# A planner that lays out two attentions on one core: its model of transfers changed, four output products ready at the end, and the V product of the first unit at other places

## The chip, the cores and the metric

The kernel runs on one core of one Trainium2 chip. The metric is the device time of a whole execution, in microseconds; the median of several executions is given with its lowest and highest. One execution was also recorded by the hardware profiler. Its span, from the first to the last recorded instruction, is a little shorter than the time of that execution.

## The reference

Two independent attentions over their own inputs, each with S = 2048 tokens, D = 1024 and 32 heads of 32 dimensions. A looks at eight keys at distances 0, 2, ..., 14 behind each query; B at the 256 keys up to and including the query. The outputs stand side by side.

```python
# A: W, dil = 8, 2
idx = pos[:, None] - (jnp.arange(W) * dil)[None, :]
kg, vg = k[:, :, idx_c, :], v[:, :, idx_c, :]
logits = jnp.where(idx >= 0, einsum("bhsd,bhswd->bhsw", q, kg) * Dh ** -0.5, -1e9)
a = einsum("bhsw,bhswd->bhsd", softmax(logits), vg) @ wo
# B: W = 256
mask = (i - j >= 0) & (i - j < W)
scores = jnp.where(mask, einsum("bhqd,bhkd->bhqk", q, k) * Dh ** -0.5, -1e9)
b = einsum("bhqk,bhkd->bhqd", softmax(scores), v) @ wo
return jnp.concatenate([a, b], axis=-1)
```

In both, q, k and v are thirds of x @ wqkv, and everything is float32.

## The kernel before, in words

**Units and slots.** The work is cut into eight units of 512 tokens. Units 0 to 3 are the chunks of B ("dense"; units 1 to 3 also need the last 256 keys of the unit before, called the halo). Units 4 to 7 are A: its tokens are sorted into even and odd, so that a step of two becomes a step of one and the window is 8 neighbouring keys; two chunks for each parity, the second of each with a halo. Each unit has eight slots of four heads (a slot's running number is hg = 8u + s).

**Arithmetic.** Float32 products are made on TensorE from two parts of each operand (a value cast to fp32r, and what the cast left), in three products (TERMS): high by high, high by low, low by high. So a weight is loaded raw (L103), cast on DVE (L129) and its rest is made by a subtraction on DVE (L137) or POOL (L134). This is the class Stream. It has three raw buffers (NRAW) and walks a fixed list of items; split_to(n) splits up to item n, and the next load is issued when a split is planned to end. An item "x" is split into two halves in xpool, an item "w" as one tile in wpool, which has three buffers. The first eight loads are issued by ACT, the others by POOL.

**A slot** runs through these steps:
1. the products for q and k (L363, 24 matmuls each), their copies out of PSUM (ACT L314 and DVE L318 into one of two buffers nat), and SP's copies of them into the stacked operands qst and kst (L328: three for q, three for k; halo copies L308 and L333). There are two of each stack; so the copies of slot hg are issued only after the last product of slot hg − 2 (dictionary `waiting`);
2. the first pass over the scores (L614, 16 matmuls), the row maximum on DVE (L619) and the sum of exponentials on ACT (L624);
3. the logarithm (L637), three small steps on DVE (up to L645), the rows' constants turned round on TensorE (L653), copied on DVE (L657) and put by SP (L660) into two more rows of qst;
4. the second pass (L696 dense, L509 window), which now gives scores less the constant, the exponentials on ACT (L701 or L514), the masks on POOL and DVE (L682, L685, L520, L524);
5. the product with V (L741 or L548), and the copy of its result into ot (ACT L577, DVE L581).

Beside them run the V product of the unit in four parts (L415, copied out through copy_out at L379 or L382) and the output product of the unit before in eight products (L455, n = 0 to 7), each copied into the one output buffer `ost` (pool stp, NST = 1) and stored by ACT (L470). V_SLOTS says after which slot's q and k products a part of V stands; O_SLOTS the same for output products. The last V part of a unit also holds the splits of the next unit's x. The last unit's output products come at the end, each over k = 0 to 7, where k needs ot of slot k; k = 7 has to wait for the last slot.

**PSUM.** Ring rg has three banks (L363, L415, L455), ring rs four (L614, L653, L696, L509), ring ro one (L741, L548).

**Order.** Everything is issued in an order that Python works out beforehand. The class Clock keeps a time at which each engine is free, and the durations given to its methods (0.95 for a stack copy, 1.9 for a raw load and so on) are estimates. The loop at L801 to L829 has four sequences: the row steps (aux), second passes with the product with V (twos), first passes (ones), and the large products (gemm). At each step it asks each sequence when its next item could start and takes the first; what follows an item (copies, masks, DMAs) is put off by `defer` to its planned time and issued in that order. So a duration in the Clock has no time on the chip, but shifts where instructions stand in the queues of the engines. Transfers have two planned queues, "copies" (from SP) and "loads" (from ACT and POOL); one that runs while the other queue is busy is made longer by half the overlap.

The tail is ordered by hand after that: the first TAIL = 2 of the last eight output products run up to k = 6, then their last steps, then the others.

Of the kernel before, what the change touches and what calls it, by code (L numbers as in the profile page):

```python
# [14 lines left out]
P = 128  # L15
NG = 8
NK = 8
# [6 lines left out]
VPARTS = ((0,2),(2,2),(4,2),(6,2))  # L24
V_SLOTS = {0: 0, 1: 1, 5: 2, 7: 3}
O_SLOTS = {2: (0, 1), 3: (2, 3), 4: (4, 5), 5: (6, 7)}
NX, NST = 10, 1
TAIL, LAND, XAT = 2, 0.45, 1
C1, C3, CG, CV = 0.114, 0.2, 0.231, 0.243
TERMS = ((0, 0), (0, 1), (1, 0))  # L30

# [1 line left out]
class Clock:  # L33
# [3 lines left out]
    SEM = 0.17  # L37

    def __init__(self):
        self.free = dict(pe=0.0, act=0.0, dve=0.0, pool=0.0, sp=0.0, copies=0.0, loads=0.0)  # L40
        self.later, self.lands = [], []
        self.n = 0

    @property
# [3 lines left out]
    def use(self, eng, dur, *ready):  # L48
        start = max((self.free[eng],) + ready)
        self.free[eng] = start + dur  # L50
        return start + dur + self.SEM

    def copy(self, dur, *ready):

        return self.move("copies", "loads", self.use("sp", 0.63, *ready, self.lane()) + 0.4, dur)

    def load(self, dur, *ready):

        return self.move("loads", "copies", self.use("act", 0.35, *ready, self.lane()) + 0.45, dur)

    def fetch(self, dur, *ready):

        t = max(self.use("pool", 1.0, *ready) + 0.6, self.free["loads"])
        self.free["loads"] = t + dur + 0.5 * max(0.0, min(2 * dur, self.free["copies"] - t))
        return self.free["loads"] + LAND

    def lane(self):

        return self.lands[-8] if len(self.lands) >= 8 else 0.0

    def move(self, q, other, t, dur):

        t = max(t, self.free[q])
        self.free[q] = t + dur + 0.5 * max(0.0, min(2 * dur, self.free[other] - t))
        self.lands.append(self.free[q] + LAND)
        return self.lands[-1]

    def defer(self, t, f):
        heapq.heappush(self.later, (t, self.n, f))
# [7 lines left out]
class Stream:  # L87
# [10 lines left out]
    def load_to(self, n):  # L98
        while self.loaded < min(n, len(self.items)):
            raw = self.raws.tile([P, 1024], F32, tag="raw", name="raw")  # L100
            ap = self.items[self.loaded][1]
            early = self.loaded < 8
            (self.nc.scalar if early else self.nc.gpsimd).dma_start(raw if len(ap.shape) == 2 else raw.rearrange("p (a b) -> p a b", a=2), ap)  # L103
            self.raw[self.loaded] = raw, (self.ck.load if early else self.ck.fetch)(1.9, self.ck.now)
            self.loaded += 1

    def split_to(self, n):
        while self.split < min(n, len(self.items)):
            i = self.split
            self.load_to(i + 1)  # L110
            raw, t0 = self.raw.pop(i)
            if self.items[i][0] == "x":
                self.tiles[i], self.ready[i] = [], []
                for h in range(2):
                    t = self.xpool.tile([P, 2, S], F32R, tag="x", name="x")
                    self.ready[i].append(self.parts(t, raw[:, h * S:(h + 1) * S], t0))
                    self.tiles[i].append(t)
            else:
                t = self.wpool.tile([P, 2, 1024], F32R, tag="w", name="w")
                self.ready[i] = self.parts(t, raw, t0)  # L120
                self.tiles[i] = t
            self.split += 1
            end = self.ready[i] if self.items[i][0] != "x" else max(self.ready[i])
            self.ck.defer(end, lambda n=i + NRAW + 1: self.load_to(n))

    def parts(self, t, raw, t0):
# [20 lines left out]
def kernel(ctx, tc, xs, wqk, wv, wo, outs, units):  # L147
# [23 lines left out]
    for u in range(U):  # L171
        for s in range(NG):
            if u and s in O_SLOTS:
                plan += [("o", u - 1, n) for n in O_SLOTS[s]]
            plan.append(("qk", u, s))
            if s in V_SLOTS:
                plan.append(("v", u, V_SLOTS[s]))
        if u + 1 < U:
            plan.append(("x", u + 1))
    plan += [("o", U - 1, n) for n in range(NG)]  # L180
# [14 lines left out]
    for p in plan:  # L195
        ly = units[p[1]][0]
        if p[0] == "o":
            item(p, "w", wo[ly, p[2]])
        elif p[0] == "v":
            s0, n = VPARTS[p[2]]  # L200
            for g in range(n):
                if n == 2:
                    item(p + (g,), "w", wv[ly, s0 + g])
                else:
                    w4 = wv[ly, s0 + g // 2:s0 + g // 2 + 3:2, :, g % 2 * 512:g % 2 * 512 + 512]
                    item(p + (g,), "w", w4.rearrange("t p c -> p t c"))
        elif p[0] == "qk":
            for t in range(2):
                if p + (t,) not in where:
                    item(p + (t,), "w", wqk[ly, 2 * p[2] + t])  # L210
        else:
            if NG - 1 in V_SLOTS:
                item(("qk", p[1], 0, 0), "w", wqk[units[p[1]][0], 0])
                unit_x(p[1])
            else:
                unit_x(p[1], 0)
                item(("qk", p[1], 0, 0), "w", wqk[units[p[1]][0], 0])
                unit_x(p[1], 1, 2, 3)
# [79 lines left out]
    def qk_items(u, s):  # L298
# [5 lines left out]
        def read_halo():  # L304
            w = 256 if dense else 128
            hb = halo[(u + 1) % 2][s]
            for r, a in enumerate((0, 1, 0)):
                nc.sync.dma_start(kst[buf][r:96:3, :, 256 - w:256].bitcast(F32), hb[:, a, 256 - w:])  # L308
                ck.copy(0.55 if dense else 0.35, ck.now)

        def evac(t, ps, bank):
            hl = natp.tile([P, 2, S], F32R, tag="nat", name="nat")
            sc = SCALE if t == 0 else 1.0
            nc.scalar.activation(hl[:, 0, :], ps, AF.Copy, scale=sc)  # L314
            r = ck.use("act", 0.48, ck.now + ck.SEM)

            def low():
                nc.vector.scalar_tensor_tensor(hl[:, 1, :], ps, sc, hl[:, 0, :].bitcast(F32), op0=ALU.mult,  # L318
                                               op1=ALU.subtract)
                e = ck.use("dve", 0.6, r)  # L320
                rg.give(bank, e)

                def stack():
                    if t == 1 and has_halo:
                        read_halo()
                    dst, c = (qst[buf], 0) if t == 0 else (kst[buf], 256)
                    for i, a in enumerate((0, 0, 1) if t == 0 else (0, 1, 0)):
                        nc.sync.dma_start(dst[i:96:3, :, c:c + S].bitcast(F32), hl[:, a, :].bitcast(F32))  # L328
                        e2 = ck.copy(0.95, e, ck.now)
                    if t == 1:  # L330
                        done["stack"][u, s] = e2
                    if t == 1 and u + 1 < U and units[u + 1][3]:
                        nc.sync.dma_start(halo[u % 2][s], hl[:, :, 256:].bitcast(F32))  # L333
                        e2 = ck.copy(0.95, e, ck.now)
                    done["nat"][hg, t] = e2

                if hg < 2 or hg - 2 in done["o"]:
                    stack()
                else:
                    waiting.setdefault(hg - 2, []).append(stack)  # L340

            ck.defer(r, low)
# [95 lines left out]
    def o_items(u, n):  # L438
        h = {}

        def ready(k):
            if (u * NG + k) not in done["ot"]:
                return None
            if k == 0:
                st.split_to(where["o", u, n] + 1)
                h["r"] = st.ready[where["o", u, n]]
                return latest(rg.when(), h["r"], done["ot"][u * NG])
            return done["ot"][u * NG + k]

        def run(k):  # L450
            if k == 0:
                h["ps"], h["b"] = rg.take()
                h["w"], _ = st.get(where["o", u, n])
            for i, (a, b) in enumerate(TERMS):
                nc.tensor.matmul(h["ps"], h["w"][:, a, k * P:(k + 1) * P], ot[u, k][:, b, :],  # L455
                                 start=(k == 0 and i == 0), stop=(k == NK - 1 and i == 2))
            if k == 3 and (u < U - 1 or n != TAIL - 1):
                st.split_to(where["o", u, n] + 2)

        def after(k):  # L460
            if k == NK - 1:
# [1 line left out]
                for f in list(stores.values()):  # L463
                    f()
                o = stp.tile([P, S], F32, tag="ost", name="ost")
                e = copy_out(o, h["ps"], h["b"], rg)

                def store():
                    if stores.pop((u, n), None):
                        nc.scalar.dma_start(outs[u, n], o)  # L470
                        ck.load(0.8, e)

                stores[u, n] = store
                ck.defer(e, store)
# [114 lines left out]
    def attention(u, s):  # L589
# [9 lines left out]
        def first(b, j):  # L599
# [18 lines left out]
            def top():  # L618
                nc.vector.tensor_tensor_reduce(ps[:, :n], ps[:, :n], mask[:, cut:full], scale=-1.0, scalar=BIG,  # L619
                                               op0=ALU.add, op1=ALU.min, accum_out=nm)  # L620
                e = ck.use("dve", (n + 80) / 960, ck.now)

                def total():
                    nc.scalar.activation(ps[:, :n], ps[:, :n], AF.Exp, bias=nm, scale=-1.0, accum_out=sm)  # L624
# [26 lines left out]
        def rows(hl):  # L651
# [4 lines left out]
            def copy():  # L656
# [1 line left out]
                e = ck.use("dve", 0.25, ck.now)  # L658
                rs.give(bank, e)
                nc.sync.dma_start(q[96:98, :, :].bitcast(F32), rt.bitcast(F32))  # L660
                h["rows"] = ck.copy(0.3, e)

            return copy

# [209 lines left out]
```

## Time and profile before

| | |
|---|---|
| median of 3 executions | 1975.59 us (1972.74 to 1976.52) |
| the profiled execution | 1973.82 us |
| its span | 1972.1 us |
| mean granted clock of TensorE | 0.987 of full speed |
| weight load / VectorE / ScalarE / GpSimd busy | 1619.8 / 1295.7 / 957.5 / 708.7 us |
| moved by DMA | 294.92 MB, mean 150 GB/s |

Busy shares by line: the costliest groups show how the work of TensorE is made up. Columns: line, engine, operation, tiles and count; then busy time and mean ns of one; then the idle time ahead of them and what ended most of it.

```profile
L363 PE MATMUL g<-x,w 128*128 128x512 f32 x3072 | 801.9, 401 | 8.6 <-DVE w L129 8.0
...
L415 PE MATMUL g<-w,x 128*128 128x256 f32 x3072 | 413.3, 285 | 0.0
...
L455 PE MATMUL g<-ot,w 128*128 128x512 f32 x1536 | 384.2, 397 | 3.6 <-DVE w L129 2.9
...
L614 PE MATMUL s<-kst,qst 96*128 96x384 f32 (+3 forms) x1024 | 238.7, 303 | 16.2 <-ACT s L624 7.1
```

Matmuls are pipelined, so the mean of one holds overlap: 24 matmuls of L363 in a row take 5.54 us, 0.231 each. The idle time stands in the last column. A time with a line behind it, as in "7.1 <-ACT s L624", says who ended most of that idle time: here TensorE waited for a bank of ring rs until ACT had summed the exponentials in it.

### The profile page before, as it was taken

The page shows a single profiled execution, that of the slowest core. Times are in us where ns is not written, and L with a number is a line of the kernel's source. Part 1 is how long each engine was busy: PE and PEld are TensorE (multiplying, and loading weights), DVE is VectorE, ACT ScalarE, POOL GpSimd, SP SyncE. Part 2 cuts the span into 40 slices and gives each one's busy share as a digit, 9 for nine tenths or more (in the row PEclk, how much of TensorE's full clock was granted, in tenths as well). Part 3 has the DMA queues.
Part 4 walks back from the last instruction along what each step waited for, and adds up shares of the span by engine and source line. Part 5 has one row for each costly group of instructions (what it writes and reads, how often), then busy time and mean ns, then how long its engine had stood idle before and what let it go on. Part 6 is the DMA issues. An engine that isn't in the chain of part 4 may idle for free.

```text
span 1972.1 us, 36479 instructions
## 1 busy us (share of the span) xinstructions
PE 1924.7 (98%) x12608; PEld 1619.8 (82%) x12608; DVE 1295.7 (66%) x3762; ACT 957.5 (49%) x3137; POOL 708.7 (36%) x923
## 2 busy tenths in 40 slices
PE   7999999999999999999999999999999999999998
PEld 6878887888877878788878888978888788888886
DVE  5687776678665786567865657655666557666653
ACT  3565554475654656555563344423534334434441
POOL 4334343444433434443443323233332333233221
PEclk9999999999999999999999999999989999999998
DMA  5555546455546465345645647455553565556442
GB/s 176 150 139 153 160 124 178 132 153 157 152 136 174 121 189 149 117 140 148 177 119 146 173 139 196 128 149 170 149 163 116 174 177 162 141 146 172 136 126 75
DMA packets 136502, 294.92 MB, mean 150 GB/s; under 512 B 14464, under 2 KB 42112, under 8 KB 136320
## 3 DMA queue, kind: packets, MB, share of 16 engines
q1 hardware_dynamic: 85632, 124.82, 26.1%
q0 software_dynamic: 40320, 146.82, 22.9%
q10 hardware_dynamic: 10368, 20.98, 2.9%
q8 instruction: 100, 1.64, 0.4%
q14 instruction: 82, 0.67, 0.1%
HBM read 163.58 MB, written 27.26 MB: 97 GB/s over the span
## 4 chain that ended last, share of the span: by engine, by line
PE 84%; DVE 7%; DMA 6%; ACT 2%; issue 1%; SPq 0%; POOL 0%; DVEq 0%; ACTq 0%; POOLq 0%
PE g L363 31%; PE g L455 16%; PE g L415 16%; PE s L614 7%; PE s L696 5%; PE o L741 4%; PE s L509 3%; DMA qst<-rt 3%; PE o L548 2%; DMA kst<-nat 1%; DMA raw<-xs 1%; DVE x L137 1%; DVE w L129 1%; ACT s L624 1%; DVE w L137 1%
## 5 line engine op out<-in xcount | busy, mean ns | idle before, releaser
L363 PE MATMUL g<-x,w 128*128 128x512 f32 x3072 | 801.9, 401 | 8.6 <-DVE w L129 8.0
L134 POOL TENSOR_TENSOR w<-raw,w 128x512 fp32r<-128x512 f32 x225 | 392.5, 1745 | 897.2 <-PE s L614 285.7
L363 PEld LDWEIGHTS g<-x,w 128*128 128x128 f32 x3072 | 562.0, 191 | 110.9 <-DVE w L129 8.4
L624 ACT ACTIVATE s<-s,nm 128x384 f32<-128x384 f32 (+3 forms) x1024 | 452.3, 443 | 231.0 <-DVE nm L619 227.1
L415 PE MATMUL g<-w,x 128*128 128x256 f32 x3072 | 413.3, 285 | 0.0
L415 PEld LDWEIGHTS g<-w,x 128*128 128x128 f32 x3072 | 392.7, 191 | 1.9 <-issue 0.6
L455 PE MATMUL g<-ot,w 128*128 128x512 f32 x1536 | 384.2, 397 | 3.6 <-DVE w L129 2.9
L455 PEld LDWEIGHTS g<-ot,w 128*128 128x128 f32 x1536 | 283.8, 190 | 58.1 <-DVE w L129 3.6
L619 DVE CUSTOM_DVE_ANT_0 s<-s,mask_d 128x384 f32<-128x384 f32 (+2 forms) x512 | 262.0, 556 | 72.9 <-PE s L614 71.5
L614 PE MATMUL s<-kst,qst 96*128 96x384 f32 (+3 forms) x1024 | 238.7, 303 | 16.2 <-ACT s L624 7.1
L701 ACT ACTIVATE pbuf<-s 128x384 f32<-128x384 f32 (+2 forms) x480 | 197.1, 507 | 85.5 <-PE s L696 81.8
L614 PEld LDWEIGHTS s<-kst,qst 96*128 96x128 f32 x1024 | 181.3, 192 | 60.5 <-ACT s L624 18.1
L624 ACT ACTIVATION_READ_ACCUMULATOR s<-s,nm 128x1 f32 x1024 | 210.2, 205 | 0.0
L619 DVE CUSTOM_DVE_ANT_0 s<-s,mask_w 128x136 f32<-128x136 f32 (+1 forms) x512 | 142.4, 322 | 98.4 <-PE s L614 96.8
L129 DVE CAST w<-raw 128x1024 fp32r<-128x1024 f32 x256 | 199.9, 781 | 9.4 <-PE g L455 9.4
L137 DVE TENSOR_TENSOR w<-raw,w 128x512 fp32r<-128x512 f32 x287 | 197.2, 696 | 8.8
L682 POOL TENSOR_SCALAR_AFFINE_SELECT pbuf<-pbuf 128x128 f32<-128x128 f32 (+1 forms) x383 | 147.9, 404 | 150.1 <-ACT pbuf L701 143.5
L314 ACT ACTIVATE nat<-g 128x512 fp32r<-128x512 f32 x128 | 76.6, 598 | 255.2 <-PE g L363 247.8
L318 DVE SCALAR_TENSOR_TENSOR nat<-g,nat 128x512 fp32r<-128x512 f32 x128 | 88.3, 690 | 145.5 <-ACT nat L314 134.9
L524 DVE TENSOR_TENSOR pbuf<-pbuf,keep_w 128x272 f32<-128x272 f32 (+1 forms) x224 | 116.9, 566 | 61.5 <-ACT pbuf L514 60.6
L619 DVE DVE_READ_ACCUMULATOR2_ANT nm<- 128x1 f32 x1024 | 144.3, 141 | 0.0
L696 PEld LDWEIGHTS s<-qst,kst 98*128 98x128 f32 x704 | 106.2, 189 | 37.8 <-PE o L741 10.0
(48 smaller groups left out, 1227.3 us busy)
## 6 DMA issues: line engine op xcount, KB each, us to landing
raw<-wqk POOLq DMA_DIRECT2D x126, 512.0 KB, 3.7
qst<-nat SPq DMA_DIRECT2D x192, 256.0 KB
kst<-nat SPq DMA_DIRECT2D x192, 256.0 KB
raw<-wo POOLq DMA_DIRECT2D x64, 512.0 KB, 3.7
raw<-wv POOLq DMA_DIRECT2D x62, 512.0 KB, 4.5
outs<-ost ACTq DMA_DIRECT2D x64, 256.0 KB
raw<-xs POOLq DMA_DIRECT2D x28, 512.0 KB, 4.8
halo<-nat SPq DMA_DIRECT2D x40, 256.0 KB
```

The lines of the kernel that those rows point to most:

```text
L129: nc.vector.tensor_copy(t[:, 0, :], raw)
L134: nc.gpsimd.tensor_tensor(o, a, b, op=ALU.subtract)
L137: nc.vector.tensor_tensor(o, a, b, op=ALU.subtract)
L363: nc.tensor.matmul(h["ps"], h["w"][:, a, k * P:(k + 1) * P], xt[u][k][:, b, :], start=(k == 0 and i == 0), stop=(k == NK - 1 and i == 2))
L415: nc.tensor.matmul(ps, xt[u][k][:, a, p0:p0 + P], h["w"][:, c, k % kw], start=(k == 0 and i == 0 and r == 0), stop=(k == NK - 1 and i == 2 ...
L455: nc.tensor.matmul(h["ps"], h["w"][:, a, k * P:(k + 1) * P], ot[u, k][:, b, :], start=(k == 0 and i == 0), stop=(k == NK - 1 and i == 2))
L614: nc.tensor.matmul(ps[:, :n], q[0:96, j, b * P:(b + 1) * P], kk[0:96, j, c0:c1], start=True, stop=True)
L619: nc.vector.tensor_tensor_reduce(ps[:, :n], ps[:, :n], mask[:, cut:full], scale=-1.0, scalar=BIG, op0=ALU.add, op1=ALU.min, accum_out=nm)
L624: nc.scalar.activation(ps[:, :n], ps[:, :n], AF.Exp, bias=nm, scale=-1.0, accum_out=sm)
L682: nc.gpsimd.affine_select(w, w, pattern=[[0, m], [step, n]], compare_op=ALU.is_ge, fill=0.0, base=base, channel_multiplier=chan)
L696: nc.tensor.matmul(ps[:, i * n:(i + 1) * n], kk[0:98, j, 256 + kb * P:256 + (kb + 1) * P], q[0:98, j, q0:q0 + n], start=True, stop=True)
L701: nc.scalar.activation(w, ps[:, :pack * n].rearrange("p (j n) -> p j n", j=pack), AF.Exp)
```

## The change

**1. The Clock's transfers.** The two planned queues are replaced by one list of busy stretches. A transfer asks for a start (the issue time plus a lead) and gets the first gap from there on that is long enough, except that it never goes ahead of one that asked for an earlier start; it runs alone, with no stretching. Every kind of transfer goes through it, the loads issued by POOL too. Their estimated durations change: a raw load 1.9 to 1.95, a stack copy 0.95 to 1.08, a halo copy of the window kind 0.35 to 0.45, the row copy 0.3 to 0.35, an output store 0.8 to 0.85. A load on POOL is planned to hold POOL for 0.6 instead of 1.0. The row maximum on DVE is planned as (n + 110) / 960 instead of (n + 80) / 960.

**2. Four output products ready at the end.** TAIL becomes 4. Product n = 3 of the last unit takes its bank from ring rs instead of rg. The weights of the last unit's products n = 3 to 7 become items "xw": they are split into two halves in xpool, with a planned time for each half. The places at which split_to is called in the last unit's products are set anew.

**3. V of the first unit.** Unit 0 has V parts after slots 0, 2, 4 and 7 (V0_SLOTS) instead of 0, 1, 5 and 7.

No product, copy or store is added or taken away, except that the five weights of "xw" are cast in two halves each.

```diff
+V0_SLOTS = {0:0,2:1,4:2,7:3}
 NX, NST = 10, 1
-TAIL, LAND, XAT = 2, 0.45, 1
+TAIL, LAND, XAT = 4, 0.45, 1
...
-        self.free = dict(pe=0.0, act=0.0, dve=0.0, pool=0.0, sp=0.0, copies=0.0, loads=0.0)
-        self.later, self.lands = [], []
+        self.free = dict(pe=0.0, act=0.0, dve=0.0, pool=0.0, sp=0.0)
+        self.later, self.lands, self.busy = [], [], []
...
+    def issue(self, eng, hold, lead, dur, *ready):
+        start = max((self.free[eng],) + ready)
+        self.free[eng] = start + hold
+        return self.move(start + lead, dur)
+
     def copy(self, dur, *ready):
-        return self.move("copies", "loads", self.use("sp", 0.63, *ready, self.lane()) + 0.4, dur)
+        self.lands.append(self.issue("sp", 0.63, 1.25, dur, *ready, self.lane()))
+        return self.lands[-1]
...
     def fetch(self, dur, *ready):
-        t = max(self.use("pool", 1.0, *ready) + 0.6, self.free["loads"])
-        self.free["loads"] = t + dur + 0.5 * max(0.0, min(2 * dur, self.free["copies"] - t))
-        return self.free["loads"] + LAND
+        return self.issue("pool", 0.6, 1.3, dur, *ready)
...
-    def move(self, q, other, t, dur):
-        t = max(t, self.free[q])
-        self.free[q] = t + dur + 0.5 * max(0.0, min(2 * dur, self.free[other] - t))
-        self.lands.append(self.free[q] + LAND)
-        return self.lands[-1]
+    def move(self, t, dur):
+        busy = self.busy = [x for x in self.busy if x[1] > self.now - 20.0]
+        i = 0
+        while i < len(busy):
+            if busy[i][1] <= t or busy[i][0] < t:
+                t = max(t, busy[i][1])
+            elif busy[i][0] - t >= dur:
+                break
+            else:
+                t = busy[i][1]
+            i += 1
+        busy.insert(i, (t, t + dur))
+        return t + dur + LAND
...
-            if self.items[i][0] == "x":
+            if self.items[i][0] != "w":
...
+            vs = V_SLOTS if u else V0_SLOTS
+            if s in vs:
+                plan.append(("v", u, vs[s]))
...
-            item(p, "w", wo[ly, p[2]])
+            item(p, "w" if p[1] < U - 1 or p[2] < 3 else "xw", wo[ly, p[2]])
...
-                        e2 = ck.copy(0.95, e, ck.now)
+                        e2 = ck.copy(1.08, e, ck.now)
...
+        last = u == U - 1
+        ring = rs if last and n == 3 else rg
...
+                h["r"] = r if isinstance(r, list) else [r, r]
+                return latest(ring.when(), h["r"][0], done["ot"][u * NG])
+            return max(done["ot"][u * NG + k], h["r"][k // 4])
...
-            if k == 3 and (u < U - 1 or n != TAIL - 1):
-                st.split_to(where["o", u, n] + 2)
+            if k == 3 and (not last or n == 0 or n > 2):
+                st.split_to(where["o", u, n] + (3 if last and n == 0 else 2))
+            if k == 5 and last and n in (1, 2):
+                st.split_to(where["o", u, n] + 3)
...
-                e = ck.use("dve", (n + 80) / 960, ck.now)
+                e = ck.use("dve", (n + 110) / 960, ck.now)
```

## The prediction

> **What bounds the kernel now.** I read the page's totals and its chain of waits first, then TensorE's waits, then windows around each wait, then the timeline.
>
> ```profile
> span 1972.1 us, 36479 instructions
> ...
> PE 1924.7 (98%) x12608; PEld 1619.8 (82%) x12608; DVE 1295.7 (66%) x3762; ACT 957.5 (49%) x3137; POOL 708.7 (36%) x923
> ...
> PE 84%; DVE 7%; DMA 6%; ACT 2%; issue 1%; SPq 0%; POOL 0%; DVEq 0%; ACTq 0%; POOLq 0%
> ```
>
> TensorE is busy 98%; 1972.1 − 1924.7 = 47.4 us are idle. The matmuls stay the same in kind and number, so only idle time, and what follows it, can change. TensorE's waits, with total, count and longest (us):
>
> ```profile
> engine line waited for: us in total, times, longest us
> PE g L363 <- DVE w L129: 8.0, 1, 8.0
> PE s L614 <- ACT s L624: 7.1, 8, 1.2
> PE s L509 <- DMA qst<-rt: 6.7, 10, 1.8
> PE s L614 <- DMA kst<-nat: 5.7, 5, 2.0
> PE s L653 <- DVE hl L645: 3.4, 10, 0.5
> PE g L455 <- DVE w L129: 2.9, 1, 2.9
> ```
>
> The 8.0 is the first load and cannot move. The rest are attention steps that reach TensorE before their data. Windows show a second price:
>
> ```profile
> core 0: us, PE busy (x) PEld busy (x) DVE busy (x) ACT busy (x) POOL busy (x), PEclk, DMA share, GB/s
> 211.50:215.00 3.50, 2.42 (x11) 1.83 (x12) 3.31 (x12) 2.62 (x12) 2.14 (x2) 0.95 0.42 136
> 1453.50:1460.00 6.50, 6.50 (x27) 5.92 (x27) 2.19 (x6) 3.54 (x12) 0.23 (x1) 0.51 0.19 70
> 1935.00:1937.50 2.50, 2.50 (x7) 1.97 (x6) 2.44 (x4) 0.00 (x0) 0.90 (x2) 0.50 0.34 85
> ```
>
> PEclk is the granted clock. In the second row TensorE is never idle, yet runs half its matmuls. Stepping such windows through the trace, the clock is at half from 33.72, 214.63 and 989.45 (3.41 us each), 1224.97 and 1685.77 (6.83), 1453.66 (10.24) and 1921.29 (17.07): 51.2 us, some 25 lost. The idle sums just before were 2.0, 1.9, 3.4, 1.8, 2.4, 2.8 and the tail's; 1.25 us at 470 and at 730 brought nothing. So I charge a stall of about 2 us with 1.7 more (3.41 at half). By the Trainium skill, page "TensorE: Matmul & The Clock Gate", section "Part 1: The HAM clock gate (the "warmup" mystery)", a whole idle window of about 3.4 us is needed to throttle. The trace agrees on the length and contradicts the trigger; taken by the rule, the sum below falls by the clock terms of its new stalls, which is the first rival.
>
> ```profile
> 33.06 0.64 PE L614 MATMUL s<-kst,qst 96*128 96x128 f32 x4 [2.01 <-DMA kst<-nat]
> ...
> 470.29 2.13 PE L614 MATMUL s<-kst,qst 96*128 96x384 f32 x4 [1.25 <-ACT s L624]
> ...
> 1453.14 0.58 PE L509 MATMUL s<-qst,kst 98*128 98x8 f32 x4 [1.80 <-DMA qst<-rt]
> ...
> 1918.07 0.67 SPq L660 DMA_DIRECT2D qst<-rt  x1
> 1920.52 3.80 PE L509 MATMUL s<-qst,kst 98*128 98x8 f32 x20 [1.36 <-DMA qst<-rt]
> ...
> 1929.08 0.59 ACT L379 COPY ost<-g 128x512 f32<-128x512 f32 x1 [2.04 <-PE g L455]
> ...
> 1931.83 0.69 DVE L382 COPY ost<-g 128x512 f32<-128x512 f32 x1 [4.06 <-DMA outs<-ost]
> 1932.43 0.69 DVE L129 CAST w<-raw 128x1024 fp32r<-128x1024 f32 x1
> ...
> 1933.17 35.35 PE L455 MATMUL g<-ot,w 128*128 128x512 f32 x144 [2.85 <-DVE w L129]
> ```
>
> Two facts to keep: a row copy takes 1920.52 − 1918.07 = 2.45 us from issue to use, and one output buffer makes the next copy wait 4.06 us, with a weight cast queued behind it, for which TensorE then waits 2.85.
>
> **The change, part by part.** The planner's new durations run nowhere on the chip; they act only by the order they produce, so I compared the two instruction orders, each distance in TensorE work (L363 0.231 us a matmul, L455 0.227, L415 0.121, L614 0.178 or 0.112).
>
> *Start (V of unit 0 spread).* Before the first L614, 84 matmuls of L415 stand instead of 60: 24 × 0.121 = 2.9 us more cover against the wait of 2.01. The wait goes, and its half-clock stretch: −2.0 − 1.7 = −3.7 (0 to −3.7). The load and split they need come earlier on DVE; that the copies slip by more than 0.9 is the bound at 0.
>
> *Inside units.* Rows to second pass (L653 to L509 or L696): ten places with 3.5 us between wait 4.3 in sum; 4.2 to 4.9 now cover nearly all: −3.9. Slot 4 of unit 0 shrinks from 5.4 to 2.8: +1.0. K product to first L614: four places gain 0.7 to 1.4: −3.1. L653 itself comes 0.7 to 3.5 earlier in four slots, later in four others: +1.8. Sum −4.2; taking only gains or only losses, −7 to +3.
>
> *Unit boundaries.* Here the last V part carries eight x splits (1.06 us of DVE each), and the order shifts. Entering unit 1: 1.5 us of work stand between rows and second pass where about 3 are needed, and banks and PV come later too: idle 2.3 → 5.0, the clock term 1.7 stays: +2.7. Entering units 2 and 3: L653 stands 0.87 us after the last L614 (4.9 before). PV's second half and ACT's copy of ot (L577) now come ahead of six exponential sums: 0.1 + 0.59 + 6 × 0.56 + about 1.0 (logarithm, DVE parts, semaphores) = 5.1, less 1.2 of TensorE work = 3.9 idle, plus 1.7 clock, where 1.25 is lost now: +4.35 each. Unit 4: 2.95 of losses become 0.5, −2.4. Units 5 and 7: +0.7 each. Unit 6: 7.9 (2.8 idle and the 10.24 at half) → 5.5, −2.4. Sum +8.0. Bounds: ACT passes the sums during the V product (then +1.5 for each of units 2 and 3, and 0 for unit 1: sum 0), or all lag is carried on, which is the third rival.
>
> *Tail.* From L653 at 1917.51 to the last matmul's end at 1968.53 are 51.0 us, for 156 × 0.227 + 20 × 0.112 + 1.2 (PV) = 38.8: 12.2 lost (1.36 rows, 0.70 ot, 2.85 weights, the rest clock). Four products ready give 21 L455 after L653 (4.8 us, row copy and parts covered), 15 amid second pass and PV, and 6 at once after PV, covering ot. Those three waits go, and the first dip. But four output copies now follow each other through the one buffer (ost), 1931.83 − 1929.08 = 2.75 us apart, and the split of weight n=5 is behind them on DVE (five wide casts become ten narrow: 0.75 us more DVE here). It is ready some 9.5 us after the copies start; TensorE arrives at 7.4: 2.1 to 2.3, plus 1.7 clock: 4.0 lost. 4.0 − 12.2 = −8.2 (no new stall −12; a stall of 4 with two dips −5).
>
> SP, POOL and ACT issue the same DMAs, so no queue gets more work, but their order moves. SP's row copy (L660) has the stack copies of L328 around it, 0.67 us an issue (the row at 1918.07): each one put ahead of it delays the second pass by that much, which the boundary terms hold as distances and the third rival as a pile. POOL issues the loads (L103) between its subtracts (L134, 1.7 us each): where one is passed by a subtract it lands that much later, covered by three raw buffers as long as the weights are split a product ahead, as they are everywhere but in the tail. What is queued behind the waiting DVE copy there is n=5's split, counted above; POOL's subtract of it follows, and the next load after that.
>
> Sum: −3.7 − 4.2 + 8.0 − 8.2 = −8.1. The profiled execution took 1973.8, of which the span is 1972.1; 1965.7 after. The median shown is 1.8 above this execution: 1967.5.
>
> **Rivals.**
>
> *The clock does not follow short stalls.* New stalls at units 1 to 3 and the tail cost no half clock, and V work hides part of the ACT queue: −1.7 × 4 = −6.8 and about −1 more: 1959.5. For: 1.25 us brought nothing. Against: 1.9 at 211 did. Chance 0.12.
>
> *The dips double.* Half clock lasted 6.83 after idle sums of 1.8 and 2.4; if so at four new stalls, +1.7 × 4 = +6.8: 1974.3, no change. Chance 0.20.
>
> *Slower: the lag at a boundary is carried into the next slot.* SP issues a copy in 0.67 us, and the stack copies of slot 7 wait until PV of slot 5 has ended. PV now being late, ten issues (6.7 us) come between it and the row copy, and the first L614 of slot 7, only 2.1 us after L653, waits 2.0 for them and brings 3.4 of clock: 5.4 at each of units 1, 2 and 3, +16: net +8, 1983 at full price, 1979 if one boundary escapes. It decides as soon as the copies land later than TensorE gets there. For: row copies at boundaries took 4.5 us from issue (1218.63 to 1223.14; 1448.71 to 1453.14), not 2.45. Against: the waits named kst<-nat sum to only 5.7 now. Beside this stands the Trainium skill, "DMA: Bandwidth & Descriptors", "Queues, rings and completion order": each DMA engine takes packets from its queues in turn, so a server in order of arrival misplaces copies just where loads run. The 4.5 against 2.45 agrees. Chance 0.26.
>
> *It does not do what it says* (TensorE follows data, not the plan, at most places): then only start and tail, −12, inside the first rival's times.
>
> **How the numbers follow.** Forecast 0.42, the others as given. What a measurement can tell from no change is 0.2%, 3.95 us. Forecast 1967.5, own range 1962 to 1973, from the in-unit and tail bounds. Faster: 0.42 and 0.12, 0.54; same: 0.20; slower: 0.26. Both signs hold much of the chance, so the range runs from 1958 (first rival, a little under) to 1981 (between the third's two prices).
>
> **What would show it.** Right: no wait on kst<-nat near 33 and no dip there; row-copy waits (10 times 6.7) cut to under 4; waits of 3 to 4 us at L653 near 470 and 730 with a half-clock stretch behind; tail of about 43 us from L653, with one stall at L455 on the cast of n=5. Wrong: clean boundaries (first rival), half clock over 6 us at 470 and 730 (second), or new waits on kst<-nat in slots 7 (third).

## The result, and the profile after

The changed kernel is slower. In 14 runs each on one chip the median went from 1972.94 us (1969.89 to 1976.96) to 1981.51 us (1977.15 to 1987.5); the ratio of the two is 1.0044, 95% interval 1.0033 to 1.0055. The forecast was a gain of 8 us; the measured loss is 8.6. The profiled execution took 1982.04, its span 1980.1.

The page's totals and chain of the changed kernel, to be read beside those of before:

```profile
span 1980.1 us, 36490 instructions
...
PE 1926.7 (97%) x12608; PEld 1620.4 (82%) x12608; DVE 1283.5 (65%) x3720; ACT 956.8 (48%) x3133; POOL 734.4 (37%) x974
...
PE 85%; DVE 6%; DMA 5%; ACT 2%; issue 2%; POOL 0%; SPq 0%; DVEq 0%; ACTq 0%; POOLq 0%
```

TensorE has the same 12608 matmul records. Idle time is 1980.1 − 1926.7 = 53.4 us instead of 47.4, and busy time is 2.0 longer. TensorE's waits in the changed kernel (L637 is the first pass, L614 before; L676 the rows, L653 before; L719 and L532 the second passes):

```profile
PE g L378 <- DVE w L143: 8.5, 3, 8.0
PE s L637 <- issue: 7.4, 4, 2.2
PE s L676 <- DVE hl L668: 7.0, 10, 2.1
PE s L637 <- DMA kst<-nat: 6.4, 5, 3.2
PE s L637 <- ACT s L647: 6.0, 7, 1.1
PE s L719 <- DMA qst<-rt: 4.3, 4, 2.0
PE s L532 <- DMA qst<-rt: 2.9, 3, 1.3
```

Row-copy waits (on qst<-rt) fell from 9.1 to 7.2, those on the bank of ring rs from 7.1 to 6.0, and the wait for a weight in the tail from 2.9 to 2.1. What grew is the first pass: 5.7 on kst<-nat became 6.4 there and 7.4 on "issue", which means that the page can name no releaser; with 0.8 more put down to L378, 14.6 us. The waits at the rows grew as well, from 4.9 to 8.5 (L653, then L676, on DVE and ACT). The first-pass waits stand here:

```profile
438.27 0.94 PE L637 MATMUL s<-kst,qst 96*128 96x384 f32 x4 [2.24 <-issue]
...
1285.50 0.64 PE L637 MATMUL s<-kst,qst 96*128 96x136 f32 x4 [2.13 <-issue]
...
1460.91 0.71 PE L637 MATMUL s<-kst,qst 96*128 96x136 f32 x4 [3.25 <-DMA kst<-nat]
...
1746.33 0.64 PE L637 MATMUL s<-kst,qst 96*128 96x136 f32 x4 [2.14 <-issue]
```

These four are the first first-pass matmuls of slot 6 of unit 1, slot 1 of unit 5, slot 7 of unit 5 and slot 1 of unit 7; smaller ones follow at 702.54, 870.31, 968.05, 1002.27, 1218.96 and 1558.24. The page names those copies into kst at five of the ten; that the others wait for them too is shown further down, where the loads are halved.

The timeline around the third shows how such copies come late. The K product ended at 1444.9:

```profile
1445.57 7.42 SPq L343 DMA_DIRECT2D kst<-nat  x3
...
1445.90 1.78 DVE L143 CAST w<-raw 128x1024 fp32r<-128x1024 f32 x1
...
1451.05 0.68 DVE L333 SCALAR_TENSOR_TENSOR nat<-g,nat 128x512 fp32r<-128x512 f32 x1
```

The low part of k (L333) stands on VectorE behind splits of weights and x, so SP's three issues stretch over 7.42 us instead of about 2. Then the copies meet loads. From 1455 to 1461 the DMA view of the changed kernel has, by queue, packets, MB and the share of all 16 engines' time:

```profile
q0 software_dynamic: 297, 1.08, 65.1%
q1 hardware_dynamic: 267, 0.48, 35.2%
```

q1 is SP's queue with the copies, q0 POOL's with the loads. The copies have a third of the engines' time. In a shorter stretch, 430.9 to 432.1, ahead of the wait at 438, they have next to nothing, though all three k copies were issued by 429.96:

```profile
q0 software_dynamic: 78, 0.32, 98.7%
q14 instruction: 1, 0.01, 1.6%
q1 hardware_dynamic: 2, 0.00, 0.2%
```

In the first stretch the last two loads were issued at 1455.14 and 1457.27, behind all three copies (the last at 1452.39), and ran while copies were still under way: from 1457 to 1460 q0 has 85.4% of the engines' time and q1 19.3%. So transfers are not served one at a time in order of arrival, as the new planner has them. The Trainium skill, page "DMA: Bandwidth & Descriptors", section "Queues, rings and completion order", has each DMA engine go round the queues that have work and drain a whole packet of one before it turns to the next. The shares of 65.1% and 35.2% fit that; whether the 1.2 us in which the copies had 0.2% are one packet of the load on each engine, no run here shows.

### The profile page after: what moved, and what is told of

It reads as the page before. It is cut to its first block, busy times and chain, and to the rows that moved or that the text cites. A ratio compares the mean times of both kernels' runs of the same rounds, so it can differ in the third digit from the quotient of the medians.

```text
span 1980.1 us, 36490 instructions
## 1 busy us (share of the span) xinstructions
PE 1926.7 (97%) x12608; PEld 1620.4 (82%) x12608; DVE 1283.5 (65%) x3720; ACT 956.8 (48%) x3133; POOL 734.4 (37%) x974
## 4 chain that ended last, share of the span: by engine, by line
PE 85%; DVE 6%; DMA 5%; ACT 2%; issue 2%; POOL 0%; SPq 0%; DVEq 0%; ACTq 0%; POOLq 0%
PE g L378 32%; PE g L476 16%; PE g L430 15%; PE s L637 7%; PE s L719 5%; PE o L764 4%; PE s L532 3%; PE o L571 2%; DMA qst<-rt 2%; DMA kst<-nat 2%; ACT s L647 1%; DVE w L143 1%; DMA raw<-xs 1%; DVE x L151 1%; DVE w L151 1%
## 5 line engine op out<-in xcount | busy, mean ns | idle before, releaser
L378 PE MATMUL g<-x,w 128*128 128x512 f32 x3072 | 806.0, 402 | 8.9 <-DVE w L143 8.5
L148 POOL TENSOR_TENSOR w<-raw,w 128x512 fp32r<-128x512 f32 x228 | 397.2, 1742 | 890.6 <-issue 350.2
L378 PEld LDWEIGHTS g<-x,w 128*128 128x128 f32 x3072 | 564.7, 192 | 113.1 <-DVE w L143 9.1
L476 PE MATMUL g<-ot,w 128*128 128x512 f32 x1416 | 356.9, 394 | 0.0
L642 DVE CUSTOM_DVE_ANT_0 s<-s,mask_d 128x384 f32<-128x384 f32 (+2 forms) x512 | 262.4, 556 | 90.5 <-PE s L637 89.5
L476 PEld LDWEIGHTS g<-ot,w 128*128 128x128 f32 x1416 | 258.1, 188 | 46.3 <-issue 0.2
L637 PE MATMUL s<-kst,qst 96*128 96x384 f32 (+3 forms) x1024 | 234.6, 304 | 21.2 <-issue 7.4
L637 PEld LDWEIGHTS s<-kst,qst 96*128 96x128 f32 x1024 | 179.9, 191 | 64.9 <-issue 24.9
L705 POOL TENSOR_SCALAR_AFFINE_SELECT pbuf<-pbuf 128x128 f32<-128x128 f32 (+1 forms) x431 | 168.9, 411 | 154.2 <-ACT pbuf L724 148.5
L642 DVE CUSTOM_DVE_ANT_0 s<-s,mask_w 128x136 f32<-128x136 f32 (+1 forms) x512 | 142.5, 322 | 117.4 <-PE s L637 116.7
L143 DVE CAST w<-raw 128x1024 fp32r<-128x1024 f32 x251 | 195.9, 780 | 0.0
L151 DVE TENSOR_TENSOR w<-raw,w 128x512 fp32r<-128x512 f32 x274 | 189.3, 698 | 8.7
L333 DVE SCALAR_TENSOR_TENSOR nat<-g,nat 128x512 fp32r<-128x512 f32 x128 | 88.3, 690 | 124.6 <-ACT nat L329 114.1
L547 DVE TENSOR_TENSOR pbuf<-pbuf,keep_w 128x272 f32<-128x272 f32 (+1 forms) x224 | 107.3, 522 | 62.1 <-ACT pbuf L537 60.6
L642 DVE DVE_READ_ACCUMULATOR2_ANT nm<- 128x1 f32 x1024 | 144.5, 141 | 0.0
L719 PEld LDWEIGHTS s<-qst,kst 98*128 98x128 f32 x704 | 109.8, 191 | 40.3 <-ACT s L647 13.6
```

The lines of the kernel that those rows point to most:

```text
L143: nc.vector.tensor_copy(t[:, 0, :], raw)
L148: nc.gpsimd.tensor_tensor(o, a, b, op=ALU.subtract)
L151: nc.vector.tensor_tensor(o, a, b, op=ALU.subtract)
L378: nc.tensor.matmul(h["ps"], h["w"][:, a, k * P:(k + 1) * P], xt[u][k][:, b, :], start=(k == 0 and i == 0), stop=(k == NK - 1 and i == 2))
L476: nc.tensor.matmul(h["ps"], w[:, a, c:c + P], ot[u, k][:, b, :], start=(k == 0 and i == 0), stop=(k == NK - 1 and i == 2))
L637: nc.tensor.matmul(ps[:, :n], q[0:96, j, b * P:(b + 1) * P], kk[0:96, j, c0:c1], start=True, stop=True)
```

## The experiments

### The three parts alone

First the parts were run one by one, and the change without its Clock. Each ratio in the tables below is to the kernel before on the same chip. In the kernels with the new tail and the old Clock, product n=3 starts only when at most three second passes are left.

```diff
 # v0_alone: before, with
+            vs = V_SLOTS if u else V0_SLOTS
 # tail_alone: before, with TAIL 4, "xw", ring rs for n=3, the new split_to places, and
+            if k == 0 and ring is rs and len(twos) - pos["2"] > 4:
+                return None
 # clock_alone: before, with the new class Clock and the new durations
 # clock_back: the changed kernel, with the old class Clock and the old durations
```

> The kernel before with V0_SLOTS alone. My theory (the new model of transfers causes the loss, because copies land later than it plans) expects little here: 60 V matmuls still stand before the first L614, so the 2.0 us wait at 33 us and the half-clock stretch behind it stay; units 1 to 7 keep their order. -3 to +3 us against the kernel before. The rival that the V product's new places cause the loss expects +5 or more, all of it before 260 us.

> The kernel before with the four ready output products alone (product n=3 held back until three second passes of the last slot are left, since the old planner would block itself otherwise). My theory: -7 us (-5 to -9), the waits of 1.36, 0.70 and 2.85 after 1917 replaced by about 1 for the row copy (2.8 us of work between rows and second pass) and about 2 for the weights of n=5 behind four output copies. The rival that four copies through one output buffer cost more than they save expects 0 or slower.

> The kernel before with the new Clock and its new durations alone. My theory: all of the loss sits here, +13 us (+9 to +18) against the kernel before: waits at first L614 behind kst copies at about 438, 703, 1002, 1285, 1461 and 1746 us as in the changed kernel, L653 waits of 2 us at two boundaries, and the old tail. The rival that tail or V places cause the loss expects 0 or faster here, since 3.9 us of row-copy waits go.

> The changed kernel with the old Clock and old durations (new tail and new V places kept; n=3 held back as in the tail run). My theory: the sum of the runs with tail alone and V places alone, -7 us (-4 to -11) against the kernel before, so some 15 us faster than the changed kernel. The rival (loss from tail or V places, or from dips of the clock that come with any new order) expects it slower than the kernel before.

| kernel | ratio to the kernel before | interval | as us of 1968 |
|---|---|---|---|
| v0_alone | 1.0032 | 1.0017 to 1.0047 | +6.3 |
| tail_alone | 0.9963 | 0.9948 to 0.9978 | −7.3 |
| clock_alone | 1.0087 | 1.0064 to 1.0110 | +17.1 |
| clock_back | 1.0006 | 0.9993 to 1.0019 | +1.2 |

The tail does what it was costed at, and the Clock carries most of the loss. The V places cost 6.3 where −3 to +3 was expected, and so clock_back, expected at −7 (−4 to −11), came out at +1.2. The profile of v0_alone shows the same kind of loss: first passes wait 11.1 us for kst<-nat in nine places, where the kernel before has 5.7 in five. The longest is 2.97 at 215.84, with 6.83 us of half clock beside it; another, 1.93, stands at 963.98, far behind the first unit. Row-copy waits fell at the same time (9.1 to 5.8), and that execution's span was only 1.6 above that of the kernel before, so the profile doesn't hold all of the 6.3. The three parts sum to +0.82%, the whole is +0.44%: in clock_alone there are waits of 3.37 at 126 and 2.80 at 212 that the changed kernel doesn't have; V places and Clock both reorder the start of the program, so their effects do not simply add.

TensorE's waits in v0_alone (L616 the first pass) and in clock_alone (L627 the first pass, L666 the rows) show the same kind of loss as in the changed kernel:

```profile
PE s L616 <- DMA kst<-nat: 11.1, 9, 3.0
...
PE s L627 <- DMA kst<-nat: 11.1, 7, 2.9
PE s L666 <- DVE hl L658: 10.3, 10, 3.4
...
PE s L627 <- issue: 4.7, 3, 2.0
```

### Are the copies late, and is it the loads?

One run leaves the order as it is and halves the load traffic. Another leaves the traffic and makes the planner believe in a later landing.

```diff
 # half_loads: the changed kernel, with
+            half = (raw[:, :512], ap[:, :512]) if len(ap.shape) == 2 else (raw[:, :512], ap[:, 0]) if ap.shape[1] == 2 else None
+            (self.nc.scalar if early else self.nc.gpsimd).dma_start(*half)
...
-        nc.vector.tensor_copy(t[:, 0, :], raw)
+            nc.vector.tensor_copy(t[:, 0, :].rearrange("p (a b) -> p a b", a=2), lo[:, None, :].to_broadcast([P, 2, 512]))
...
 # stack_margin: the changed kernel, with
-                        done["stack"][u, s] = e2
+                        done["stack"][u, s] = e2 + 2.5
```

> The changed kernel with its order untouched, but each raw load moves only its first half (256 KB) and both halves of a weight or of x are made from that: the second half of every x and weight row is left out of the computation. If loads that share the DMA engines with the k copies make them late, the waits at first L614 (14.6 us) fall to under 7, those at about 438, 1002, 1285, 1461 and 1746 by about 1 us each, and some half-clock stretches with them: -2 to +4 us against the kernel before. If the copies are late because SP issues them late (row copy and halo copies ahead of them, k's low part late on VectorE), these waits stay above 11 and the run is +5 to +9.

> The changed kernel, but the planner believes that the k copies of every slot land 2.5 us later than its model says, so that first passes are placed later behind other work. My theory (the first passes lose because copies land later than the new model plans, and the order leaves no slack): the waits at first L614, 14.6 us in ten places in the changed kernel, fall below 5, with most of the four half-clock stretches behind them; 6 to 14 us faster than the changed kernel, so -5 to +3 us against the kernel before. The rival (the stall only moves to L653 and the second pass, since too little other work is left) expects no gain: +6 to +11 us, with waits at L653 and on qst<-rt grown by as much.

half_loads: ratio 0.9883 (0.9863 to 0.9903), −23 us against the kernel before. stack_margin: 0.9914 (0.9894 to 0.9933), −17. Both gained far more than I expected. Two lines of TensorE's waits for half_loads, where L642 is the first pass:

```profile
PE s L642 <- issue: 3.0, 3, 1.8
...
PE s L642 <- DMA kst<-nat: 0.3, 1, 0.3
```

In the same order, with the same issues on SP, 14.6 us of first-pass waits became 3.3. VectorE was no less busy (1283.3 us beside 1283.5), so it is the transfers that became shorter. The waits on "issue" shrank along with those on kst<-nat, so they were waits for copies. Most of what stays is at slot 1 of units 5 and 7 (0.87 and 1.80), where SP issues the k copies 3.5 us after the K product's last matmul instead of 1.05, behind the row copy and the halo copies: that part is SP's order, not the loads. Row copies gained too (7.2 to 2.2 in sum), so not all of the gain is that of the first pass, and 1.1 is that of the very first load. No run halves the loads of the kernel before, so how much of the −23 that kernel would gain too is not known; what names the cause is the waits, not the time. For stack_margin:

```profile
span 1951.7 us, 36482 instructions
...
PE 1912.4 (98%) x12608; PEld 1607.1 (82%) x12608; DVE 1291.6 (66%) x3710; ACT 956.5 (49%) x3135; POOL 728.5 (37%) x982
...
PE s L637 <- DMA kst<-nat: 0.9, 1, 0.9
```

With 0.8 on "issue" its first-pass waits are 1.7 us. Idle time falls by 14.1 (53.4 to 39.3), and busy time by 14.3: half clock falls from ten stretches (51.2 us) to three (10.2). That second part was larger than I had counted on. Waits at L676 go from 8.5 to 7.3 and those on row copies from 7.2 to 4.5: the stall did not move there.

The planner's own times can be printed from the code. From the end of the K product to the planned landing of its copies, beside the trace's time from the start of that product's last matmul (0.4 us before its end) to the first pass that waited:

| slot | planned landing | changed kernel | half_loads |
|---|---|---|---|
| unit 1, slot 6 | 13.8 | 15.1 | 13.0 (no wait) |
| unit 3, slot 7 | 30.1 | 33.0 | 31.0 (no wait) |
| unit 5, slot 1 | 8.7 | 11.3 | 10.1 |
| unit 5, slot 7 | 12.2 | 16.4 | 13.5 |
| unit 7, slot 1 | 8.7 | 11.3 | 11.0 |

The plan sets the first pass at 0.1 to 0.6 us behind its planned landing in all five. Without slack each lateness is a stall. The kernel before had hardly more slack: its planner sets 42 of its 64 first passes less than 0.6 us behind the planned landing, that of the changed kernel 46. What grew is the lateness: at the places that waited, the first pass began more than 2 us behind the planned landing once before (slot 0 of unit 0, 2.5) and four times after (slot 7 of unit 3, slots 1 and 7 of unit 5, slot 1 of unit 7).

### How much slack, and does the model matter?

```diff
 # tail_two: tail_alone, with
-                o = stp.tile([P, S], F32, tag="ost", name="ost")
+                if last:
+                    o = natp.tile([P, 2, S], F32R, tag="nat", name="nat")[:, 0, :].bitcast(F32)
...
 # margins: tail_two, with
+                        done["stack"][u, s] = e2 + (3.0 if u + s == 0 else 0.0)
+                h["rows"] = ck.copy(0.3, e) + 0.7
 # margin_two: stack_margin, with outputs as in tail_two
 # margin_less: margin_two, with 1.2 in place of 2.5
 # margin_rows: margin_two, with
+                h["rows"] = ck.copy(0.35, e) + 0.5
 # old_margin: tail_two (the old Clock), with
+                        done["stack"][u, s] = e2 + 2.5
```

> The run with the tail alone, with the last unit's outputs put through the two buffers of nat, free by then, in place of the one output buffer. My theory of the tail (n=5's weights stand on VectorE behind output copies that wait for the one buffer): the 2.1 us stall at L455 and the half-clock stretch behind it vanish, 3.8 us less than with the tail alone, -11 us (-9 to -13) against the kernel before. The rival (the load of n=5's weights is late itself) expects the stall to stay.

> The run before this one, with the old planner believing that the k copies of the very first slot land 3.0 us later and that each row copy lands 0.7 us later. Expected if slack at these two places is what the old planner lacked: the 2.0 at 33 us with its dip goes (-3.7) and the waits on qst<-rt inside units (4.3 us in ten places) fall below 1.5: -15 to -20 us against the kernel before. The rival: a shifted greedy order makes new stalls at unit boundaries, as the changed Clock did, and gives back 5 to 15: -10 to 0.

> The run with 2.5 us of margin for the k copies, with the last unit's outputs through the two buffers of nat as in the tail run. If what stands behind output copies is what makes n=5's weights late, the 2.13 at L455's line after 1931 us goes, and its half-clock stretch if there is one: 2 to 4 us less than with the margin alone, -18 to -22 us against the kernel before. The rival (the last stretch is set by something else) expects -15 to -18.

> The run with margin and two output buffers, with 1.2 us of margin in place of 2.5. Copies were late against the new plan by 1.3 (slot 1.6), 2.6 (5.1 and 7.1), 2.9 (3.7) and 4.2 (5.7). If the loss is lateness against plan, place by place, 1.2 us covers the first and leaves about 1.4, 1.7 and 3.0 at the others, with their half-clock stretches: -5 to -14 us against the kernel before, worse than with 2.5. If any small slack does, it is as fast as with 2.5.

> The run before this one, with row copies also believed to land 0.5 us later. With the margin alone, waits on qst<-rt sum to 4.3 us, 2.7 of it at two places near 200 us with a half-clock stretch. If slack is the general rule, they go: 3 to 5 us less than the run before this one. The rival: the planner reorders everything else, and new waits at L653 or at unit boundaries give it back: 0 to +8 against the run before this one.

> The kernel before with the new tail (n=3 held back, outputs through nat) and the OLD Clock, but with the k copies believed to land 2.5 us later. If the gain of the margin is the slack alone, whatever model of transfers stands under it, this comes to -16 to -22 us against the kernel before, like the new Clock with the margin. If the new model of transfers also helps where loads and copies meet, this stays behind by 4 or more: -8 to -13 (the run of the tail with two buffers had -13).

| kernel | ratio to the kernel before | interval |
|---|---|---|
| tail_two | 0.9934 | 0.9912 to 0.9956 |
| margins | 0.9909 | 0.9877 to 0.9942 |
| margin_two | 0.9883 | 0.9846 to 0.9921 |
| margin_less | 0.9877 | 0.9846 to 0.9908 |
| margin_rows | 0.9864 | 0.9832 to 0.9896 |
| old_margin | 0.9913 | 0.9880 to 0.9947 |

By these ratios all are faster than both kernels; margin_rows, the fastest by its median (1946.34 us beside 1974.69 for the kernel before on that chip), is 1.36% below the kernel before.

- tail_two: −13 us, at the far end of its range, with an interval from −9 to −17. The wait for the weights of n=5 is gone, so they stood behind output copies that waited for the one buffer. In the run with the tail alone the cause is plain to see:

```profile
1939.55 0.69 DVE L382 COPY ost<-s 128x512 f32<-128x512 f32 x1 [2.18 <-DMA outs<-ost]
1940.16 0.42 DVE L129 CAST x<-raw 128x512 fp32r<-128x512 f32 x1
...
1940.63 0.73 PE L463 MATMUL g<-ot,x 128*128 128x512 f32 x2 [2.13 <-DVE x L129]
```

- margins: slack at the start and for the row copies brings what was expected (−18 us), and the first wait shrinks from 2.0 to 0.57 with no half clock behind it; row-copy waits are 1.4 in all. Part of that is paid back: the first passes of the other slots wait 7.8, in tail_two 5.4.
- margin_two: the same wait is gone here too; −23 us with an interval from −16 to −30, so what the two buffers add to the margin is not settled.
- margin_less: the expectation place by place fell. With 1.2 us of slack the run is as fast as with 2.5, and the waits ahead of the slots' first first-pass matmuls are 1.3 us in sum. A changed belief moves the whole order, so the five late places of the table don't come back as they were.
- margin_rows: waits on row copies fall from 5.1 to 1.4 in the lines by releaser, those of the rows matmul rise from 8.3 to 12.2; the gain over margin_two lies within the two intervals.
- old_margin: −17 beside −23 for margin_two, with intervals that overlap, and the two profiled spans agree (1953.2). So with slack both planners come out about equal, and whether the new model is worth anything then stays open. For the new Clock slack is the larger part: it turns +0.44% into −0.86% (stack_margin). For the old Clock a gain from slack is not shown: tail_two has −13 without it, and the intervals overlap.

## Why the prediction was wrong

- **The step that failed** is "K product to first L614: four places gain 0.7 to 1.4: −3.1". For the places that waited before, it held: their waits fell from 3.9 to 0.84. But the term stood for every first pass outside the start, and it put new waits at nothing. Nine slots that had not waited now wait 13.7 in sum, so 3.9 became 14.6: +10.7 instead of −3.1. That is an error of 13.8, against a miss of 16.7 in all, and half clock of 3.41 us follows four of these waits. I took the distance in TensorE work as cover and left the landing where it was. At slot 7 of unit 5 the distance grew from 7.9 to 13.1, and the first pass still waited 3.25: VectorE's splits stood ahead of k's low part, and the last k copy was issued 7.9 after the start of the K product's last matmul instead of 2.4. At slot 1 of units 5 and 7 the distance grew from 8.7 to 9.2, but SP issued the copies 2.5 later, behind its row copy. In the run with halved loads 14.6 became 3.3, so the larger part of the lateness is that of loads on the same DMA engines. At three of the nine (slot 6 of units 1 and 2, slot 3 of unit 3) the distance itself shrank, by 1.4 to 2.7, which the comparison of the two orders should have counted.
- **The start** gained what was said: the wait of 2.01 at 33 and its dip are gone. The cause was wrong: v0_alone still waits 1.91 there, clock_alone does not, so the 84 matmuls come from the new Clock.
- **Row copies** inside units: right in the main. The ten places with 4.3 us fell to 0.7; slot 4 of unit 0 lost 1.6 (1.0 forecast). Over the whole program they fell only from 9.1 to 7.2, since 2.0 stands at the boundary of unit 1 and 2.6 at those of units 5 and 7.
- **Boundaries**: units 2 and 3 were forecast at 3.9 of idle time plus 1.7, and lost 0.91 + 2.08 + 0.29 = 3.3 and 0.91 + 2.07 + 0.23 = 3.2, with 3.41 and 6.83 at half clock. Unit 1 was forecast too dear: 2.00 and one dip instead of 5.0 and one. Unit 4 was forecast at 0.5 and lost 0.65 at the rows, then 1.72 at slot 7 of unit 3 with half clock of 3.41. At units 5 and 7 the idle time hardly moved (1.8 to 2.3, and 2.4 to 2.2), but half clock lasts 10.24 instead of 6.83. At unit 6 the 10.24 is gone; 1.0 idle is left, beside the 3.25 at slot 7 of unit 5.
- **The tail**: right. The stall was forecast as 2.1 to 2.3 with one dip and is 2.10 at 1958.00 with one of 3.41; the whole part, forecast at −8.2, measured −7.3 alone (interval −4 to −10).
- **The rivals**: the third had the right condition, copies that land later than TensorE gets there. Its price (+8) came out right by luck, since it was made of stalls of 5.4 at slot 7 when units 1, 2 and 3 are entered, behind SP's queue, and slot 7 of units 0, 1 and 2 does not wait at all. Slot 7 of unit 3 does (its copies were issued 21 us after the K product, when PV of slot 5 had ended); most of the others are elsewhere, and halved loads remove most of them. The sentence on queues that stood beside it named the cause that half_loads then showed.

## What to carry to other kernels

Count cover from both ends: when an order changes, ask not only how much work lies ahead of the consumer, but what now stands ahead of the producer on every queue that it passes. A planner that sets consumers right behind a predicted landing makes every error of its model a stall; here the retuned model alone made the kernel 0.9% slower, and with 1.2 us of disbelief, the new tail and a second output buffer it was 1.2% faster (tail and buffer without it: 0.7%). With two kinds of transfer on the same DMA engines, test their share by shrinking one of them and leaving the order alone.

## What the runs showed of the hardware

All half-clock stretches of an execution start on one grid of 3.41 us. In the changed kernel they start at 208.64, 471.46, 734.29, 1003.94, 1232.64, 1287.25 and so on: differences of 77, 77, 79, 67 and 16 times 3.413. Windows laid on that grid show that the place of a stall counts:

```profile
core 0: us, PE busy (x) PEld busy (x) DVE busy (x) ACT busy (x) POOL busy (x), PEclk, DMA share, GB/s
433.92:437.33 3.41, 2.10 (x10) 1.41 (x8) 0.00 (x0) 0.00 (x0) 1.73 (x2) 1.00 0.84 182
437.33:440.74 3.41, 2.47 (x16) 2.37 (x17) 2.02 (x7) 0.80 (x2) 0.00 (x0) 1.00 0.32 125
1283.84:1287.25 3.41, 1.75 (x30) 1.65 (x34) 1.41 (x9) 0.82 (x4) 0.00 (x0) 1.00 0.04 13
```

The stall of 2.24 us ahead of 438.27 falls on the border of two windows, 1.31 idle in one and 0.94 in the other, and no half clock follows. The stall of 2.13 ahead of 1285.50 lies mostly in one (1.66 idle), and 3.41 us at half clock follow. In the changed kernel each window with over 1.6 us idle was followed by a stretch and none with less. That is no border for other executions: in the kernel before, windows with 1.25 (from 1221.56) and 1.28 (from 211.22) idle were enough, while one with 1.78 in clock_back (from 1939.75) and one with 1.88 in clock_alone (from 1451.27) were followed by none, and in stack_margin stretches follow windows with 0.99 and 0.12. What else decides it is open.

So my price of 1.7 for "a stall of about 2 us" depends in part on where the stall falls on the grid. One reading behind it was wrong, too: ahead of the half clock from 989.45 TensorE was idle for 1.4 us, not 3.4, and its stall of 1.25 was as long as those at 470 and 730 that brought nothing. The Trainium skill, page "TensorE: Matmul & The Clock Gate", section "Part 1: The HAM clock gate (the "warmup" mystery)", calls the window free-running, and the grid agrees; that a window must be idle as a whole does not: less than half was enough.
